# Seven half products: the order of weight sums, sums of h and reads of the products

## The chip, the cores and the metric

The kernel runs on one core of one Trainium2 chip. The metric is the device time of one execution in microseconds (us), taken as the median of the runs. TensorE (PE) does the matrix products and transposes, VectorE (DVE) and ScalarE (ACT) the elementwise work, GpSimd (POOL) and SyncE (SP) mostly issue DMAs. Each engine works through its own queue in order.

## What is computed

```python
def _attn_ref(q, k, v):                       # 4 batches, 12 heads, 448 rows, width 64
    scores = scale * np.matmul(q, k.transpose(0, 1, 3, 2)) - np.log(S)
    attn = 1.0 / (1.0 + np.exp(-scores))
    return np.matmul(attn, v)

def _moe_ref(x, w1, w2, w3, w_out):           # 1792 tokens, 768 -> 768
    h = np.maximum(np.maximum(x @ w1, x @ w2), x @ w3)
    return h @ w_out

def _moe2_ref(x, modality_id, w_gate, modality_bias, w1, w2):
    logits = x @ w_gate + modality_bias[modality_id]
    e_idx = np.argmax(logits, axis=1)         # one of 8 experts for each token
    ...
    h = np.maximum(x[mask] @ w1[e], 0.0)      # 768 -> 1024
    out[mask] = gate_w[mask, None] * (h @ w2[e])   # 1024 -> 768
```

The three stages follow each other. The change lies in the last one, the experts.

## The kernel before

**Tiles and steps.** The last stage sorts the tokens by expert into four token tiles of 512, 512, 448 and 384 rows (the loop over `todo`, tile `i` = 0 to 3). Each tile uses one expert. In tiles 0 to 2 a tile is 26 steps `n`. Steps 0 to 11 are the first layer (`mm1`): four groups `q` of three steps, each group one quarter of h in a PSUM accumulator `hacc`. Steps 12 to 25 are the second layer, `h @ w2`, done as seven products of half size (a Strassen-like scheme) instead of eight: product `j` takes steps 12 + 2j and 13 + 2j (`mm2_prod`, tile `oacc`), 12 matmuls a step. The last tile has a plain second layer and isn't touched. All operands are split into a high and a low part (`split`: the high part by ACT in line 188, the low part by DVE in line 189), and each product is high*high + high*low + low*high.

**Operands of the seven products.** `PRODS` names the left factor (a quarter of h or a sum of quarters), the weight factor (a quarter of w2 or a sum of quarters), the PSUM accumulator group, and whether the product starts the group:

```python
SUMS = {"T1": ("B12", "B11"), "T2": ("B22", "T1"), "T3": ("B22", "B12"), "T4": ("B21", "T2")}
PRODS = (("A11", "B11", 0, True), ("S2", "T2", 1, True), ("A12", "B21", 0, False), ("S3", "T3", 1, False),
         ("S1", "T1", 2, True), ("A22", "T4", 3, True), ("S4", "B22", 2, False))
```

The quarters of w2 lie in `raw` and `rawb`; T1, T3 and T4 are written over B11, B12 and B21, T2 into `tw`. Each sum is two DVE subtractions of 128x768 (`make_sum`, line 823). The sums of h come from `half_sums`, called when a group `q` ends: groups 0 and 1 give A11 (high and low) and the start of the sums; groups 2 and 3 give A12, A22, S2 (high and low) and S1, S4 for later. S1, S3, S4 are split later by `split_sum` into the places of S2, A11 and A12.

**Reads.** Groups 0, 1 and 2 of `oacc` take two products each, and the sum is read out after the first (`read_prod(0)`, `(1)`, `(4)`) and again after the second. The second product of a group adds onto the first, so it can't start before the read of the first is done. Reads 0 and 2 are ACT's (lines 936 to 939), reads 1, 3, 4, 5, 6 DVE's (line 943).

**What sets the order.** The order on PE, ACT and DVE is the order of the code. At the end of step `n` the loop does: transposes of the next tile's tokens, if `n` is in `steps` (`gather_T`, lines 788, 796, 797); `split_sum`, if `n - 12` is in `parts`; `read_prod` at even steps from 14 on; the weight split for the step four ahead (`ahead`, `ck_split`); and the weight sums of `make[n]`. Six buffers `wo_ck` hold split weights.

```python
steps = {N1 + 4: 0, N1 + 7: 1, N1 + 10: 2}          # N1 = 12
make = {8: (("T1", 0),), 9: (("T2", 0), ("T1", 1)), 10: (("T2", 1), ("T3", 0)), 11: (("T3", 1),),
        N1 + 1: (("T4", 0),), N1 + 4: (("T4", 1),)}
parts = {2: ("S3", 0), 3: ("S3", 1), 5: ("S1", 0), 6: ("S1", 1), 8: ("S4", 0), 9: ("S4", 1)}
```

The loads of w2 for tiles 1 and 2 are issued on SP in the second layer of the tile before, those for tile 0 at fixed steps of tile 0's first layer (`wl`).

## Time and profile before

| | |
|---|---|
| median of 3 runs | 756.77 us (756.66 to 757.22) |
| profiled execution, its own time | 760.69 us |
| its span, first to last instruction | 758.9 us |
| busy, share of the span | PE 97%, DVE 64%, ACT 35%, POOL 9% |
| second layer of tile 0 | 520.88 to 560.37 us, 39.49 us |
| second layer of tile 1 | 593.05 to 632.64 us, 39.59 us |
| second layer of tile 2 | 662.39 to 702.28 us, 39.89 us |

The page's busy shares are averages over the whole span. The stretches of the table are read from PE's instructions in order of time: each ends where the next tile's first layer begins. A wait in brackets stands at the instruction that ended it, with the instruction that released it; where several were waited for, the name is that of the last by the profile.

### The profile page before, as it was taken

The numbers are of one execution on the slowest core, as the hardware profiler recorded it, in microseconds if no ns is written. First come the engines' busy times: TensorE is split into PE (matmuls) and PEld (weight loads), VectorE is DVE, ScalarE is ACT, GpSimd is POOL, SyncE is SP. The second block draws the span as 40 slices with busy tenths as digits, with TensorE's granted clock in tenths as the row PEclk, the third lists the DMA queues.
The fourth block names the chain that finished last, engine by engine and source line by source line (L and its number), as shares of the span: only waits on it lengthen the run. The fifth ranks groups of instructions, "written<-read, shape, count | busy, mean of one in ns | idle before, by whom it ended". The sixth has DMA issues, their size and how long they took to land.

```text
span 758.9 us, 10678 instructions
## 1 busy us (share of the span) xinstructions
PE 733.0 (97%) x4164; PEld 619.8 (82%) x4164; DVE 486.9 (64%) x845; ACT 262.9 (35%) x410; POOL 71.5 (9%) x96
## 2 busy tenths in 40 slices
PE   9999999999999999999999999998999799979996
PEld 6455544898998989898899888887988798979996
DVE  4777774757968878744156571338953985588463
ACT  5666555001000100100046242434623553365252
POOL 2000000000000000000010034440140013000101
PEclk9999999999999999999999999999999999989999
DMA  8866680132621312200001145483360044405101
GB/s 208 205 170 161 162 226 1 44 124 84 205 85 44 103 64 84 84 2 0 1 15 58 56 127 170 119 281 148 112 223 0 1 144 170 167 1 179 56 1 60
DMA packets 42330, 78.58 MB, mean 104 GB/s; under 512 B 6201, under 2 KB 28794, under 8 KB 42276
## 3 DMA queue, kind: packets, MB, share of 16 engines
q1 hardware_dynamic: 38420, 66.10, 28.3%
q0 software_dynamic: 3776, 11.63, 4.7%
q8 instruction: 35, 0.57, 0.3%
q14 instruction: 19, 0.16, 0.1%
q10 hardware_dynamic: 80, 0.11, 0.0%
HBM read 69.79 MB, written 11.58 MB: 107 GB/s over the span
## 4 chain that ended last, share of the span: by engine, by line
PE 87%; DVE 5%; ACT 3%; issue 2%; DMA 2%; POOL 0%; POOLq 0%; ACTq 0%; SPq 0%; DVEq 0%
PE acc L499 34%; PE hacc L898 13%; PE oacc L924 8%; PE X L344 7%; PE s L318 7%; PE acc_b L563 5%; PE acc_a L563 4%; PE oacc L912 3%; ACT wo_ck L188 2%; PE X L352 1%; PE s L334 1%; PE acc_c L563 1%; DVE wo_ck L189 1%; PE xT L788 1%; DVE hx L863 1%
## 5 line engine op out<-in xcount | busy, mean ns | idle before, releaser
L499 PE MATMUL acc<-xR,w_ring 128*128 128x512 f32 (+1 forms) x864 | 208.2, 362 | 0.0
L499 PEld LDWEIGHTS acc<-xR,w_ring 128*128 128x128 f32 x864 | 157.6, 188 | 17.7 <-issue 0.7
L898 PE MATMUL hacc<-xh,wo_ck 128*128 128x512 f32 (+3 forms) x600 | 121.9, 363 | 0.0
L898 PEld LDWEIGHTS hacc<-xh,wo_ck 128*128 128x128 f32 x600 | 107.2, 188 | 13.3 <-issue 0.3
L924 PE MATMUL oacc<-wo_ck,hx 128*128 128x384 f32 x504 | 99.1, 353 | 15.4 <-ACT wo_ck L188 8.7
L924 PEld LDWEIGHTS oacc<-wo_ck,hx 128*128 128x128 f32 x504 | 92.4, 199 | 19.2 <-ACT wo_ck L188 11.2
L499 PE MATMUL acc<-xLa,w_ring 128*128 128x512 f32 (+1 forms) x360 | 101.3, 362 | 0.0
L301 ACT ACTIVATE at<-s,nlns 128x896 f32<-128x896 f32 x84 | 78.0, 1008 | 44.9 <-PE s L318 43.6
L189 DVE TENSOR_TENSOR wo_ck<-raw,wo_ck 128x512 fp32r<-128x512 f32 (+1 forms) x87 | 67.8, 805 | 25.1 <-ACT wo_ck L188 22.4
L499 PEld LDWEIGHTS acc<-xLa,w_ring 128*128 128x128 f32 x360 | 66.3, 188 | 7.1
L188 ACT ACTIVATE wo_ck<-raw 128x512 fp32r<-128x512 f32 (+1 forms) x87 | 59.8, 725 | 18.5 <-PE oacc L924 9.0
L318 PEld LDWEIGHTS s<-kq 64*128 64x128 f32 x432 | 38.1, 187 | 21.0 <-issue 15.5
L318 PE MATMUL s<-kq 64*128 64x448 f32 x432 | 51.5, 379 | 0.0
L503 ACT ACTIVATE hA<-acc 128x1024 f32<-128x1024 f32 (+1 forms) x8 | 7.4, 923 | 118.3 <-PE acc L499 118.3
L480 DVE SCALAR_TENSOR_TENSOR gk<-wof,gk 128x768 f32<-128x768 f32 x48 | 45.9, 957 | 1.4
L989 POOL MEMSET xo<- 128x544 f32 x5 | 2.6, 550 | 411.4 <-PE acc_a L563 382.9
L775 POOL DMA_INDIRECT xg<-x2d,idx x30 | 31.6, 1053 | 77.5 <-PE xT L788 38.4
L344 PE MATMUL X<-at,u 128*64 128x448 f32 x192 | 37.8, 543 | 0.0
L370 DVE CAST xR<-X 128x448 fp32r<-128x448 f32 x24 | 14.9, 620 | 32.6 <-PE X L352 32.6
L505 DVE TENSOR_TENSOR hB<-hB,acc 128x1024 f32<-128x1024 f32 (+1 forms) x8 | 8.7, 1087 | 39.5 <-PE acc L499 39.4
L188 ACT ACTIVATE w_ring<-cv 128x768 fp32r<-128x768 f32 x14 | 11.8, 841 | 54.7 <-PE acc L499 54.7
L505 DVE TENSOR_TENSOR hA<-hA,acc 128x1024 f32<-128x1024 f32 (+1 forms) x16 | 17.4, 1086 | 20.3 <-PE acc L499 19.9
(259 smaller groups left out, 885.5 us busy)
## 6 DMA issues: line engine op xcount, KB each, us to landing
stage<-in_moe_w_dram SPq DMA_DIRECT2D x18, 768.0 KB
raw<-in_moe_w_dram SPq DMA_DIRECT2D x12, 1024.0 KB
u<-in_qk_dram SPq DMA_DIRECT2D x46, 224.0 KB
raw<-in_moe_w_dram SPq DMA_DIRECT2D x12, 768.0 KB
stage<-in_moe_w_out_dram SPq DMA_DIRECT2D x6, 768.0 KB
x2d<-xo SPq DMA_DIRECT2D x28, 128.0 KB
gk<-wgT SPq DMA_DIRECT2D x8, 384.0 KB
rawb<-in_moe_w_dram SPq DMA_DIRECT2D x4, 768.0 KB
```

What stands on the lines that cost most here:

```text
L188: nc.scalar.activation(out=r(dR), in_=src, func=ACTF.Copy)
L189: nc.vector.tensor_tensor(out=r(dL), in0=src, in1=dR, op=ALU.subtract)
L301: nc.scalar.activation(out=dst, in_=s[:, :, 0:S], func=ACTF.Sigmoid, scale=qscale, bias=nlns)
L318: nc.tensor.matmul(s[g][:, h, 0:S], r(kt[p, a, 0, 128 * g:128 * (g + 1)]), r(kt[p, x, 1]), start=(n == 0), stop=(n == 2))
L344: nc.tensor.matmul(X_t[u][64 * h:64 * h + 64, 0:S], vt[:, 2 * g + h], at[:, 2 * g + h], start=(g == 0), stop=False)
L480: nc.vector.scalar_tensor_tensor(out=junk, in0=wof[kb], scalar=1.0, in1=wgb[e % 2], op0=ALU.mult, op1=ALU.mult, accum_out=gw[:, kb, e:e + 1])
L499: nc.tensor.matmul(acc[:, c, 0:cw], r(m[:, a, kk, :]), r(x[kk][:, c0 + cw * c:c0 + cw * (c + 1)]), start=(kk == 0 and n == 0), stop=(kk == ...
L505: nc.vector.tensor_tensor(out=dst, in0=dst, in1=acc[:, :, 0:cw], op=ALU.max)
L563: nc.tensor.matmul(acc, r(hs[:, a, kk, :]), r(w(kk, b)), start=(kk == 0 and n == 0), stop=(kk == KB - 1 and n == 2))
L775: d = nc.gpsimd.indirect_dma_start(out=xg[s][:, XC[c][0]:XC[c][1]], out_offset=None, in_=x2d[c], in_offset=bass.IndirectOffsetOnAxis(ap=ix ...
L898: st["mm"] = nc.tensor.matmul(acc[:, f, t0:t1], r(w[a][:, k, 128 * f:128 * (f + 1)]), r(x[:, 2 * c + k, t0:t1]), start=(t0 == 0 and c == 0 ...
L924: nc.tensor.matmul(o[:, s, 0:HC], r(hz[k][:, x, 2 * c + f, 128 * s:128 * (s + 1)]), r(w[a][:, f]), start=(first and c == 0 and f == 0 and ...
```

## The change

Four things move; no matmul, split or sum is added or left out.

- `SUMS`: T3 = B22 - B12 comes first, then T2 = T3 + B11, T1 = B22 - T2, T4 = B21 - T2. T3 and T2 no longer need B11's place, so in tiles 1 and 2 they are formed at steps 5 to 7, T1 at steps 9 and 10. In tile 0, T3 and T2 are formed at steps 9 and 10, T1 at 12 and 13. T4 moves from steps 13 and 16 to 17 and 18.
- `half_sums`: for groups 2 and 3 only S2 is formed at once (function `s2`), with ACT's high parts of A12 and A22. The low part of A12, the sums S1 and S4 and the low part of A22 go into the queue `later`: for group 2 it is emptied at once, for group 3 one entry at each of the steps 12 to 15.
- In the second layer's steps the read comes first, then `split_sum`, then one entry of `later`, then the transposes; the transposes move from steps 16, 19, 22 to 19, 21, 23, the split of S4 from 20, 21 to 21, 22.
- Tile 0's loads of w2 are issued one place earlier each.

```diff
-        SUMS = {"T1": ("B12", "B11"), "T2": ("B22", "T1"), "T3": ("B22", "B12"), "T4": ("B21", "T2")}
+        SUMS = {"T3": ("B22", "B12"), "T2": ("T3", "B11"), "T1": ("B22", "T2"), "T4": ("B21", "T2")}
...
-            nc.vector.tensor_tensor(out=d, in0=a, in1=b, op=ALU.subtract)
+            nc.vector.tensor_tensor(out=d, in0=a, in1=b, op=ALU.add if k == "T2" else ALU.subtract)
...
-        hz, hr = {}, {}
+        hz, hr, later = {}, {}, deque()
...
+            def s2():
+                ve_(out=S2[:, :, b_], in0=b, scalar=0.0, in1=S3[:, :, b_], op0=ALU.max, op1=ALU.subtract)
+                if n2 < TH:
+                    nc.vector.tensor_scalar(out=S2[:, :, n2:TH], in0=S3[:, :, n2:TH], scalar1=-1.0, scalar2=None, op0=ALU.mult)
+                act(out=r(z("S2", 0)), in_=S2, func=ACTF.Copy)
+                act(out=r(z("A12", 0)), in_=a, func=ACTF.Relu)
+                act(out=r(z("A22", 0)[:, :, b_]), in_=b, func=ACTF.Relu)
+                nc.vector.tensor_tensor(out=r(z("S2", 1)), in0=S2, in1=z("S2", 0), op=ALU.subtract)
...
-                return
-            act(out=r(z("A12", 0)), in_=a, func=ACTF.Relu)
-            ve_(out=S1[:, :, b_], in0=b, scalar=0.0, in1=S2[:, :, b_], op0=ALU.max, op1=ALU.add)
-            ve_(out=S2[:, :, b_], in0=b, scalar=0.0, in1=S3[:, :, b_], op0=ALU.max, op1=ALU.subtract)
-            if n2 < TH:
-                nc.vector.tensor_scalar(out=S2[:, :, n2:TH], in0=S3[:, :, n2:TH], scalar1=-1.0, scalar2=None, op0=ALU.mult)
-            act(out=r(z("S2", 0)), in_=S2, func=ACTF.Copy)
-            act(out=r(z("A22", 0)[:, :, b_]), in_=b, func=ACTF.Relu)
-            ve_(out=S4, in0=a, scalar=0.0, in1=S2, op0=ALU.max, op1=ALU.subtract)
-            low("A12", a)
-            low("A22", b, n2)
-            nc.vector.tensor_tensor(out=r(z("S2", 1)), in0=S2, in1=z("S2", 0), op=ALU.subtract)
+                return []
+            s2()
+            return [lambda: low("A12", a),
+                    lambda: ve_(out=S1[:, :, b_], in0=b, scalar=0.0, in1=S1[:, :, b_], op0=ALU.max, op1=ALU.add),
+                    lambda: ve_(out=S4, in0=a, scalar=0.0, in1=S2, op0=ALU.max, op1=ALU.subtract),
+                    lambda: low("A22", b, n2)]
...
-                half_sums(q, acc, nt)
+                later.extend(half_sums(q, acc, nt))
+                while q < 3 and later:
+                    later.popleft()()
...
-        steps = {N1 + 4: 0, N1 + 7: 1, N1 + 10: 2}
+        steps = {N1 + 7: 0, N1 + 9: 1, N1 + 11: 2}
...
+        make = [{9: "T3 0 T2 0", 10: "T3 1 T2 1", 12: "T1 0", 13: "T1 1"},
+                {5: "T3 0", 6: "T2 0 T3 1", 7: "T2 1", 9: "T1 0", 10: "T1 1"}]
+        for m in make:
+            m.update({17: "T4 0", 18: "T4 1"})
...
-            if i == 0 and p in (3, 4, 6, 7):
+            if i == 0 and p in (2, 3, 5, 6):
...
+            if not last and n >= N1:
+                if n > N1 and (n - N1) % 2 == 0:
+                    read_prod((n - N1) // 2 - 1, i, ixs[i])
+                if n - N1 in parts:
+                    split_sum(*parts[n - N1])
+                if later:
+                    later.popleft()()
+                if n == NCW - 1:
+                    read_prod(6, i, ixs[i])
             if not last and n in steps:
...
```

The lines below show what stands in DVE's queue. L189 is the low part of a split (`wo_ck` a weight step, `hx` a sum of h), L823 a half of a weight sum, L863 a low part of A11, A12 or A22; `sum` and `sums` are S1 to S4, `raw` and `tw` the weights.

DVE in tile 1, around the end of group 2 of the first layer (the first of L874 to L880), before:

```order
L189 TENSOR_TENSOR wo_ck<-raw,wo_ck 128x512 x3
L874 SCALAR_TENSOR_TENSOR sums<-hacc,sum_3927 128x512
L875 SCALAR_TENSOR_TENSOR sum_3927<-hacc,sums 128x512
L880 SCALAR_TENSOR_TENSOR sum_3926<-hacc,sum_3927 128x512
L863 SCALAR_TENSOR_TENSOR hx_3785<-hacc,hx_3785 128x512
L863 SCALAR_TENSOR_TENSOR hx_3923<-hacc,hx_3923 128x512
L883 TENSOR_TENSOR hx_3784<-sum_3927,hx_3784 128x512
L189 TENSOR_TENSOR wo_ck<-raw,wo_ck 128x768
L823 TENSOR_TENSOR raw<-raw 128x2x384
L189 TENSOR_TENSOR wo_ck<-raw,wo_ck 128x768
L823 TENSOR_TENSOR tw<-raw 128x768
L823 TENSOR_TENSOR raw<-raw 128x2x384
```

The same place now; group 2 ends at L866:

```order
L189 TENSOR_TENSOR wo_ck<-raw,wo_ck 128x512
L823 TENSOR_TENSOR raw<-raw 128x2x384
L189 TENSOR_TENSOR wo_ck<-raw,wo_ck 128x512
L823 TENSOR_TENSOR tw<-raw 128x768
L823 TENSOR_TENSOR raw<-rawb,raw 128x2x384
L189 TENSOR_TENSOR wo_ck<-raw,wo_ck 128x512
L823 TENSOR_TENSOR tw<-raw 128x768
L866 SCALAR_TENSOR_TENSOR sum_3927<-hacc,sums 128x512
L872 TENSOR_TENSOR hx_3784<-sum_3927,hx_3784 128x512
L863 SCALAR_TENSOR_TENSOR hx_3785<-hacc,hx_3785 128x512
L884 SCALAR_TENSOR_TENSOR sums<-hacc,sums 128x512
L885 SCALAR_TENSOR_TENSOR sum_3926<-hacc,sum_3927 128x512
```

The four operations of T3 and T2 have moved ahead of the end of group 2, between the weight splits of the first layer.

DVE in tile 1, around the first DVE read of the second layer (L943, read 1), before:

```order
L823 TENSOR_TENSOR raw<-raw,tw 128x2x384
L189 TENSOR_TENSOR hx_3783<-sums,hx_3783 128x512
L189 TENSOR_TENSOR wo_ck<-raw,wo_ck 128x768
L189 TENSOR_TENSOR hx_3783<-sums,hx_3783 128x512
L189 TENSOR_TENSOR wo_ck<-raw,wo_ck 128x768
L797 TENSOR_TENSOR xh<-xT,xh 128x2x256 x2
L943 SCALAR_TENSOR_TENSOR xo<-oacc,gcol,xo 128x384 x2
L189 TENSOR_TENSOR wo_ck<-raw,wo_ck 128x768
```

The same place now; the read is L948:

```order
L189 TENSOR_TENSOR hx_3783<-sums,hx_3783 128x512
L885 SCALAR_TENSOR_TENSOR sum_3926<-hacc,sum_3927 128x512
L189 TENSOR_TENSOR wo_ck<-raw,wo_ck 128x768
L189 TENSOR_TENSOR hx_3783<-sums,hx_3783 128x512
L863 SCALAR_TENSOR_TENSOR hx_3923<-hacc,hx_3923 128x512
L189 TENSOR_TENSOR wo_ck<-raw,wo_ck 128x768
L948 SCALAR_TENSOR_TENSOR xo<-oacc,gcol,xo 128x384 x2
L189 TENSOR_TENSOR wo_ck<-raw,wo_ck 128x768
```

The transposed tokens (L797) and T4 (the first row before) no longer stand ahead of the read; two of the put-off operations of group 3 (L885, L863) do.

DVE in tile 0, from the weight split of step 15 to the split of S3, before:

```order
L189 TENSOR_TENSOR wo_ck<-tw,wo_ck 128x768
L823 TENSOR_TENSOR raw<-rawb,raw 128x2x384
L189 TENSOR_TENSOR wo_ck<-raw,wo_ck 128x768
L189 TENSOR_TENSOR wo_ck<-rawb,wo_ck 128x768
L823 TENSOR_TENSOR raw<-raw,tw 128x2x384
L189 TENSOR_TENSOR hx_3783<-sums,hx_3783 128x512
```

The same place now:

```order
L189 TENSOR_TENSOR wo_ck<-tw,wo_ck 128x768
L863 SCALAR_TENSOR_TENSOR hx_3785<-hacc,hx_3785 128x512
L189 TENSOR_TENSOR wo_ck<-raw,wo_ck 128x768
L823 TENSOR_TENSOR raw<-raw,tw 128x2x384
L884 SCALAR_TENSOR_TENSOR sums<-hacc,sums 128x512
L189 TENSOR_TENSOR wo_ck<-rawb,wo_ck 128x768
L823 TENSOR_TENSOR raw<-rawb,tw 128x2x384
L189 TENSOR_TENSOR hx_3783<-sums,hx_3783 128x512
```

In tile 0 both halves of T1 stand here, where the second half of T3 and the first of T4 stood; L863 and L884 are put-off operations of group 3.

## Rows read from the trace of the kernel before

**Rows 1.** The page, part 1: busy us, share of the span, instructions.
```profile
PE 733.0 (97%) x4164; PEld 619.8 (82%) x4164; DVE 486.9 (64%) x845; ACT 262.9 (35%) x410; POOL 71.5 (9%) x96
```

**Rows 2.** Waits of PE from 500 us: total us, times, longest.
```profile
PE oacc L924 <- ACT wo_ck L188: 8.7, 8, 2.0
PE oacc L924 <- DVE wo_ck L189: 6.0, 3, 2.0
PE oacc L924 <- DVE xo L943: 0.7, 1, 0.7
```

**Rows 3.** PE in order of time, second layer of tile 1: start us, busy us, instruction.
```profile
593.05 6.43 PE L924 MATMUL oacc<-wo_ck,hx 128*128 128x384 f32 x36
601.34 0.61 PE L924 MATMUL oacc<-wo_ck,hx 128*128 128x384 f32 x2 [1.85 <-ACT wo_ck L188]
603.99 5.63 PE L924 MATMUL oacc<-wo_ck,hx 128*128 128x384 f32 x22 [2.05 <-DVE wo_ck L189]
609.46 1.03 PE L788 MATMUL xT<-ident,xg 128*128 128x128 f32 x8
610.26 2.35 PE L924 MATMUL oacc<-wo_ck,hx 128*128 128x384 f32 x12
613.22 4.40 PE L924 MATMUL oacc<-wo_ck,hx 128*128 128x384 f32 x24 [0.61 <-ACT wo_ck L188]
...
628.40 4.40 PE L924 MATMUL oacc<-wo_ck,hx 128*128 128x384 f32 x24 [0.68 <-ACT wo_ck L188]
632.64 29.91 PE L898 MATMUL hacc<-xh,wo_ck 128*128 128x448 f32 x144
```

**Rows 4.** PE in order of time, ends of the second layers of tiles 0 and 2.
```profile
520.88 6.43 PE L924 MATMUL oacc<-wo_ck,hx 128*128 128x384 f32 x36
...
560.37 32.84 PE L898 MATMUL hacc<-xh,wo_ck 128*128 128x512 f32 x144
...
662.39 6.41 PE L924 MATMUL oacc<-wo_ck,hx 128*128 128x384 f32 x36
...
702.28 25.12 PE L898 MATMUL hacc<-xh,wo_ck 128*128 128x384 f32 x144
```

**Rows 5.** Stretches: length, busy of PE, PEld, DVE, ACT, POOL, PEclk, DMA share, GB/s.
```profile
604.00:606.00 2.00, 2.00 (x6) 2.00 (x7) 2.00 (x3) 2.00 (x5) 0.00 (x0) 0.50 0.00 0
482.00:484.20 2.20, 0.46 (x5) 0.22 (x3) 0.63 (x2) 0.00 (x0) 1.40 (x1) 1.00 0.87 258
```

**Rows 6.** DVE in order of time, tile 1.
```profile
588.33 0.69 DVE L880 SCALAR_TENSOR_TENSOR sum<-hacc,sum 128x512 f32<-128x512 f32 x1 [1.19 <-ACT hx L879]
588.93 1.28 DVE L863 SCALAR_TENSOR_TENSOR hx<-hacc,hx 128x512 fp32r<-128x512 f32 x2
...
592.59 0.95 DVE L189 TENSOR_TENSOR wo_ck<-raw,wo_ck 128x768 fp32r<-128x768 f32 x1
593.46 0.95 DVE L823 TENSOR_TENSOR tw<-raw 128x768 f32<-128x768 f32 x1
...
602.99 0.95 DVE L189 TENSOR_TENSOR wo_ck<-tw,wo_ck 128x768 fp32r<-128x768 f32 x1
...
611.94 1.13 DVE L943 SCALAR_TENSOR_TENSOR xo<-oacc,gcol,xo 128x384 f32<-128x384 f32 x2
```

**Rows 7.** ACT in order of time, tile 1.
```profile
585.09 0.60 ACT L873 ACTIVATE hx<-hacc 128x512 fp32r<-128x512 f32 x1 [5.51 <-PE hacc L898]
...
599.44 0.63 ACT L878 ACTIVATE hx<-sum 128x512 fp32r<-128x512 f32 x1 [3.60 <-DVE sum L875]
...
600.45 0.83 ACT L188 ACTIVATE wo_ck<-tw 128x768 fp32r<-128x768 f32 x1
```

**Rows 8.** The same places in tile 0 (ACT) and tile 2 (DVE).
```profile
512.76 0.60 ACT L873 ACTIVATE hx<-hacc 128x512 fp32r<-128x512 f32 x1 [1.12 <-PE hacc L898]
...
650.74 1.90 DVE L189 TENSOR_TENSOR wo_ck<-raw,wo_ck 128x512 fp32r<-128x512 f32 x3 [0.86 <-ACT wo_ck L188]
```

**Rows 9.** A stretch of tile 1's first layer, columns as in Rows 5.
```profile
570.00:575.00 5.00, 5.00 (x24) 4.14 (x23) 2.98 (x5) 1.42 (x3) 0.00 (x0) 1.00 0.00 0
```

More of the change, by code (lines that the diff above doesn't have):

```diff
@@ L863, in low @@
                 ve_(out=r(z(k, 1)[:, :, 0:n]), in0=src, scalar=0.0, in1=z(k, 0)[:, :, 0:n], op0=ALU.max, op1=ALU.subtract)
+            def s2():
[6 more added lines that the diff above has]
+                nc.vector.tensor_tensor(out=r(z("S2", 1)), in0=S2, in1=z("S2", 0), op=ALU.subtract)
             if q < 2:
-                act(out=S2[:, :, b_], in_=b, func=ACTF.Relu)
+                act(out=S1[:, :, b_], in_=b, func=ACTF.Relu)
                 act(out=r(z("A11", 0)), in_=a, func=ACTF.Relu)
-                ve_(out=S3[:, :, b_], in0=acc[:, :, b_], scalar=0.0, in1=S2[:, :, b_], op0=ALU.max, op1=ALU.subtract)
+                ve_(out=S3[:, :, b_], in0=acc[:, :, b_], scalar=0.0, in1=S1[:, :, b_], op0=ALU.max, op1=ALU.subtract)
                 low("A11", a)
@@ L1106, in attn_moe_kernel @@
         early = []
-        steps = {N1 + 4: 0, N1 + 7: 1, N1 + 10: 2}
-        make = {8: (("T1", 0),), 9: (("T2", 0), ("T1", 1)), 10: (("T2", 1), ("T3", 0)), 11: (("T3", 1),),
-                N1 + 1: (("T4", 0),), N1 + 4: (("T4", 1),)}
-        parts = {2: ("S3", 0), 3: ("S3", 1), 5: ("S1", 0), 6: ("S1", 1), 8: ("S4", 0), 9: ("S4", 1)}
+        steps = {N1 + 7: 0, N1 + 9: 1, N1 + 11: 2}
[3 more added lines that the diff above has]
+            m.update({17: "T4 0", 18: "T4 1"})
+        parts = {2: ("S3", 0), 3: ("S3", 1), 5: ("S1", 0), 6: ("S1", 1), 9: ("S4", 0), 10: ("S4", 1)}
         for p, (i, n) in enumerate(todo):
@@ L1160, in attn_moe_kernel @@
                     keep_gate(i + 1, SH // 128 if i + 1 == NF else NB)
-            if not last and n >= N1:
-                if n - N1 in parts:
-                    split_sum(*parts[n - N1])
-                if n > N1 and (n - N1) % 2 == 0:
-                    read_prod((n - N1) // 2 - 1, i, ixs[i])
-                if n == NCW - 1:
-                    read_prod(6, i, ixs[i])
             ahead(p + 1 + LA)
-            for k in () if last else make.get(n, ()):
-                make_sum(*k)
+            m = [] if last else make[min(i, 1)].get(n, "").split()
+            for k, c in zip(m[::2], m[1::2]):
+                make_sum(k, int(c))
             if i == NF - 2 and n == NCW - 1:
```

## The prediction

> **What bounds the kernel now.** I read the page's busy shares first, then PE's waits, then PE, DVE and ACT in order of time through one second layer, then the clock. PE is busy 97% of the span [rows 1], so only its waits, and matmuls at a low clock, can be won back. From 500 us on PE waits 15.4 us in all, every time at the second layer's matmuls (L924) [rows 2]. Each of the three changed tiles has the same four waits; tile 1 shows them [rows 3]. After 36 matmuls it waits 1.85 us and, two matmuls later, 2.05 us: step 15 needs the high and then the low part of its weights, T2, which ACT and DVE deliver at 601.28 and 603.94 [rows 6, 7]. Then 0.61 us at step 18 and 0.68 us at step 24. The profile names ACT there, but the work that fits is a read: step 18 adds onto the accumulator that read 1 empties, that read ends at 611.94 + 1.13 = 613.07 [rows 6], and PE starts 0.15 us later; the read stands behind the transposed tokens in DVE's queue.
>
> A fifth loss is no wait. The 22 matmuls after the second wait take 609.46 - 603.99 = 5.47 us; the last 24 of the stage take 632.64 - 628.40 = 4.24, or 0.1767 each, by which 22 take 3.89. [...] That costs 1.6 us.
>
> **What there is to win.** A second layer is 168 matmuls, 29.7 us at 0.1767, and three transposes of 0.80 (609.46 to 610.26), 32.1 in all. Tile 1 takes 632.64 - 593.05 = 39.6, tile 0 39.5, and tile 2, whose transposes are three quarters as large (an estimate, 1.8 for the three, 31.5 in all), 39.9 [rows 3, 4]. So 7.5, 7.4 and 8.4 us are lost, **23.3 us** together. This is more than the 15.4 of waits because of the clock and because each restart costs some 0.2 us beyond the wait shown.
>
> **The change, part by part.** Instruction counts stay, so the question is when DVE, now the last to deliver, gets to the things that PE needs. I follow its queue by hand, with the times from one start to the next: 0.60 us for an operation of 512 columns (588.33 to 588.93), 0.87 for one of 768 (592.59 to 593.46) [rows 6], and two ACT operations in 1.01 (599.44 to 600.45) [rows 7].
>
> *Sums of weights early, tile 1.* T3 and T2 are four operations of 0.87, 3.5 us, put among the first layer's splits. Group 2 ends at 585.09 [rows 7], and DVE has room before it (in the stretch of [rows 9] it is busy 2.98 of 5 us), so the first layer's matmuls hide them. What they need is loaded: no DMA moves from 570 to 575, and the first sum comes at about 580. If that cover were gone, each us of a late load would be a us for the splits queued behind it, and PE waits for those.
>
> *Only S2 at once.* From 585.09: L866 0.69, ACT's copy 0.63, L872 at 586.46. The low part of A12 must then wait for both of ACT's reads of the accumulator (1.01 for the copy and the first, 0.6 for the second), to 587.43. L880 shows that: it uses nothing that ACT's L879 writes, yet is released by it [rows 6]. [...]
>
> On from 587.43: four operations of 0.60, then two splits and two halves of T1 with step 14's split between them, 5 x 0.87: group 3's L866 starts at 594.18. S2 is ready for ACT at 594.90; three ACT operations (1.51) and step 15's high part (0.83) end at 597.24; its low part runs 597.26 to 598.2. PE wants step 15 at 593.05 + 36 x 0.1767 = 599.4. **The two large waits go**, with 1.2 us to spare, and with them the low clock.
>
> *Late next: read 1.* From 597.26 DVE has the splits of steps 15 to 19 (5 x 0.87) and six operations of 0.60 (put-off parts of group 3 and the two halves of S3), some 0.05 of waits between: read 1 starts at 605.26, ends 1.13 later at 606.39, and step 18 starts at 606.53. PE is ready at 593.05 + 72 x 0.1767 = 605.77, so it waits **0.8 us**. Step 24's wait goes: its read comes before the transposes and 1 us before PE. The stage loses 0.8 instead of 7.5.
>
> *Tile 2.* DVE is later here. Step 9's low part starts at 650.74 [rows 8]; three splits of 0.60 and the four new sums of 0.87 end at 656.02, about 1 us after group 2 does (three steps of 29.91 / 12 before 662.39 [rows 3, 4]). Walked on in the same way (some operations of this shorter tile take 0.47), step 15's weights come at 668.7, as PE wants them (662.39 + 6.36), and read 1 lets PE on at 676.83. PE is ready at 662.39 + 12.72 = 675.11: it waits **1.7 us** instead of losing 8.4.
>
> *Tile 0.* Here T3 and T2 stay between groups 2 and 3 and T1 falls between step 15 and read 1. From 512.76 [rows 8] the same walk gives step 15's low part at 527.87 (T2 waits for T3, the split of T2 for ACT), then 5 x 0.87 + 6 x 0.60 + 2 x 0.87 for T1: read 1 from 537.56, step 18 at 538.83. PE is ready at 520.88 + 12.72 = 533.60: it still loses **5.2 us** of its 7.4. Part falls at step 15, the last stretch is some 3 us without a break. Does the clock fall? It fell after 1.85 and 2.05 us of waiting with two matmuls between [rows 3]; it stayed at full after a single wait of 1.75 us at 482 [rows 5] and after all of the short ones. Three us is nearer to the first, so I take a fall and its 1.6 us; from the other row it is nothing.
>
> *At nothing.* Transposes, put-off parts, T4 and the split of S4 have 2 us or more before the step that needs them. POOL has to issue four scatters of tile 0 ahead of the last gather for tile 2, which PE uses some 50 us later. Tile 0's loads start a step earlier (32.84 / 12 = 2.7 us [rows 4]) and share the DMA queues with the gathers there: between nothing and those 2.7 us, taken at nothing, since PE waits for no gather in that tile now [rows 2].
>
> **The sum.** Lost after: 5.2 + 1.6 + 0.8 + 1.7 = 9.3 of 23.3, so **14.0 us** gained. The profiled execution took 760.69 us (758.9 of span), which gives 746.7; the median of the runs is 756.77, which gives **742.8 us**.
>
> **The rivals.**
> - *Every wait closes.* DVE reaches read 1 before PE in all three tiles: 23.3 us, 733.5. For it: in tile 1 only 0.8 us is missing. Against: in tile 0 5 us are, and nothing in the queue gets shorter.
> - *DVE falls further behind.* Tiles 1 and 2 leave no slack in DVE from the end of group 2 to read 1. If each restart there costs 1 us more and the clock falls in both (2 x 1.6), 5.2 us of the gain go: 748.0. For it: tile 2's step 15 has nothing to spare. Against: single waits under 2 us left the clock alone [rows 5].
> - *Slower: the early sums wait for loads.* T3 in tiles 1 and 2 needs the last of w2 at 580, some 13 us before the first T2 did (593.46 [rows 6]). If a load landed later than the sum's turn at 580, the splits of steps 10 to 12 would stand behind it and the first layer would stop. The kernel gets slower when loads land more than 7 us after that in tile 1 and alike in tile 2, which eats the 14.0 us; at 10 us each, it would be 756.77 - 14.0 + 20 = 762.8. Against: DMA is still at 570 [rows 9].
> - *It changes nothing that counts:* the waits return whole behind other operations, 756.8. Against: the queue has 3.5 us less before read 1, and the transposes are out of its way.
>
> **How the numbers follow.** Forecast 742.8 (740 to 746, the clock in tile 0 and 1 us of read 1 either way): 0.62. Every wait closes: 0.11. Further behind (746 to 750): 0.20. Slower: 0.03. No change: 0.04. The range 737 to 749 holds the forecast, nearly all of the second rival and the gap towards the first; outside lie the first, the slower one and no change, 0.18. Faster by over 0.2%, which is about what a measurement of this kernel can tell from none (below 755.3): 0.93; within 0.2%: 0.04; slower: 0.03.
>
> **What would show it.** Right: in tiles 1 and 2 no wait at step 15, granted clock 1.00 throughout, one wait of 0.5 to 2 us at step 18, released soon after DVE's first read; the read at about 606 (tile 1); none at step 24; second layers of 33 to 34 us in tiles 1 and 2 and 37 to 39 in tile 0, with one wait of some 3 us at step 18 there, and a clock of 0.50 behind it. Wrong: waits in the first layer (late loads), a wait at step 15 in tile 1 (ACT's queue was misread), or a read 1 that PE doesn't wait for.

## The result

The changed kernel takes **743.74 us** (median of 4 runs, 743.2 to 744.5), the kernel before beside it 756.71 (756.35 to 757.22): a ratio of 0.9829, 95% interval 0.9812 to 0.9846, 13.0 us faster. The forecast was 742.8 in a range of 737 to 749. The profiled execution took 743.39 us, its span 741.6.

The page's first part of the kernel after, as [rows 1]. PE's busy time fell by 6.5 us, although it runs the same 4164 matmuls:

```profile
PE 726.5 (98%) x4164; PEld 615.7 (83%) x4164; DVE 486.7 (66%) x845; ACT 262.9 (35%) x410; POOL 70.4 (9%) x96
```

What PE waits for from 470 us on, as [rows 2] (total us, times, longest). 15.4 us have become 7.3, and most of it is what the prediction named as next: read 1, now line L948, three times.

```profile
PE oacc L929 <- DVE xo L948: 5.4, 3, 3.1
PE oacc L929 <- ACT wo_ck L188: 0.9, 1, 0.9
PE oacc L929 <- ACT xo L942: 0.6, 2, 0.3
PE oacc L929 <- DVE wo_ck L189: 0.4, 1, 0.4
```

PE in order of time through the three second layers (tiles 0, 1, 2), as [rows 3, 4] (start us, busy us, instruction, idle time before it and its releaser; L929 was L924, L901 was L898):

```profile
517.18 6.43 PE L929 MATMUL oacc<-wo_ck,hx 128*128 128x384 f32 x36
524.51 0.62 PE L929 MATMUL oacc<-wo_ck,hx 128*128 128x384 f32 x2 [0.90 <-ACT wo_ck L188]
525.50 2.01 PE L929 MATMUL oacc<-wo_ck,hx 128*128 128x384 f32 x10 [0.37 <-DVE wo_ck L189]
527.86 4.46 PE L929 MATMUL oacc<-wo_ck,hx 128*128 128x384 f32 x24 [0.34 <-ACT xo L942]
535.45 5.96 PE L929 MATMUL oacc<-wo_ck,hx 128*128 128x384 f32 x24 [3.14 <-DVE xo L948]
...
556.40 32.84 PE L901 MATMUL hacc<-xh,wo_ck 128*128 128x512 f32 x144
589.08 12.67 PE L929 MATMUL oacc<-wo_ck,hx 128*128 128x384 f32 x72
602.61 4.40 PE L929 MATMUL oacc<-wo_ck,hx 128*128 128x384 f32 x24 [0.86 <-DVE xo L948]
...
622.02 29.91 PE L901 MATMUL hacc<-xh,wo_ck 128*128 128x448 f32 x144
651.77 8.49 PE L929 MATMUL oacc<-wo_ck,hx 128*128 128x384 f32 x48
660.49 4.43 PE L929 MATMUL oacc<-wo_ck,hx 128*128 128x384 f32 x24 [0.22 <-ACT xo L942]
666.28 4.40 PE L929 MATMUL oacc<-wo_ck,hx 128*128 128x384 f32 x24 [1.36 <-DVE xo L948]
...
684.99 25.12 PE L901 MATMUL hacc<-xh,wo_ck 128*128 128x384 f32 x144
```

In tile 1 the stage starts with 72 matmuls without a break, steps 12 to 17; then comes one wait of 0.86. In tile 0 the broken start and the long wait at step 18 remain, and the 24 matmuls behind that wait take 5.96 us instead of 4.40. The lengths of the stages (from one L929 start to the next L901 start):

| second layer, us | before | after | gained | predicted gain |
|---|---|---|---|---|
| tile 0 | 39.49 | 39.22 | 0.27 | 7.4 - 6.8 = 0.6 |
| tile 1 | 39.59 | 32.94 | 6.65 | 6.7 |
| tile 2 | 39.89 | 33.22 | 6.67 | 6.7 |
| sum | 118.97 | 105.38 | **13.59** | **14.0** |

The profiled executions differ by 760.69 - 743.39 = 17.30, the medians by 12.97. The other 3.70 us lie ahead of tile 0's second layer (520.88 before, 517.18 after): the profile of before has a wait of 1.75 us for a gather at 484 and three stalls at 466 to 468 that the profile of after lacks. An experiment below shows that these are not the change's. So the stages are what is compared here.

The groups of these matmuls by line, before and after, say how the gain divides (busy us, mean ns | idle time before them and its releasers): 15.4 - 7.2 = 8.2 us of waits and 99.1 - 93.7 = 5.4 us of busy time, together the 13.6. Of the 5.4, 4.2 us are the lower clock: before, the 22 matmuls behind the second wait took 5.65, 5.63 and 6.71 us in the three tiles, at a granted clock of 0.70 in tile 0 (531.6 to 537.2 us), 0.50 in tile 1 (604 to 606 us [rows 5]) and 0.50 in tile 2 (673.3 to 677 us), against 4.08 at a granted clock of 1.00 (601 to 605 us in the first experiment below), and after, 1.56 are lost in tile 0. The other 1.2 would be the restarts, 12 before and 7 after; that is not shown.

```profile
L924 PE MATMUL oacc<-wo_ck,hx 128*128 128x384 f32 x504 | 99.1, 353 | 15.4 <-ACT wo_ck L188 8.7 <-DVE wo_ck L189 6.0 <-DVE xo L943 0.7
```

```profile
L929 PE MATMUL oacc<-wo_ck,hx 128*128 128x384 f32 x504 | 93.7, 341 | 7.2 <-DVE xo L948 5.4 <-ACT wo_ck L188 0.9 <-ACT xo L942 0.6
```

Stretches of the kernel after, columns as in [rows 5]: in tile 1, around its wait, the clock stays at 1.00; in tile 0, behind the 3.14 us, it is 0.57 in the mean (0.50 from 536 to 538 us). DVE works without a pause in both (4.00 of 4.00).

```profile
602.00:606.00 4.00, 3.39 (x20) 3.42 (x21) 4.00 (x6) 1.59 (x4) 0.00 (x0) 1.00 0.37 98
535.00:539.00 4.00, 3.55 (x12) 3.58 (x13) 4.00 (x6) 0.40 (x1) 0.00 (x0) 0.57 0.42 117
```

DVE of the kernel after in tile 1, as [rows 6]: the last halves of T3 and T2 among the weight splits; then the end of group 2, a put-off part of group 3, and read 1.

```profile
578.22 0.95 DVE L823 TENSOR_TENSOR raw<-rawb,raw 128x768 f32<-128x768 f32 x1
579.09 0.68 DVE L189 TENSOR_TENSOR wo_ck<-raw,wo_ck 128x512 fp32r<-128x512 f32 x1
579.69 0.95 DVE L823 TENSOR_TENSOR tw<-raw 128x768 f32<-128x768 f32 x1
581.12 0.69 DVE L866 SCALAR_TENSOR_TENSOR sum<-hacc,sums 128x512 f32<-128x512 f32 x1 [0.48 <-PE hacc L901]
...
583.48 0.69 DVE L863 SCALAR_TENSOR_TENSOR hx<-hacc,hx 128x512 fp32r<-128x512 f32 x1 [0.28 <-ACT hx L871]
...
593.31 0.96 DVE L189 TENSOR_TENSOR wo_ck<-tw,wo_ck 128x768 fp32r<-128x768 f32 x1 [1.01 <-ACT wo_ck L188]
...
599.86 0.68 DVE L863 SCALAR_TENSOR_TENSOR hx<-hacc,hx 128x512 fp32r<-128x512 f32 x1
600.46 0.95 DVE L189 TENSOR_TENSOR wo_ck<-raw,wo_ck 128x768 fp32r<-128x768 f32 x1
601.33 1.14 DVE L948 SCALAR_TENSOR_TENSOR xo<-oacc,gcol,xo 128x384 f32<-128x384 f32 x2
```

DVE has 0.48 us of room before group 2 ends, so the early sums cost nothing in this tile; no sum waits for a load. Tile 2 has no such room: there the sums end about 1 us behind group 2, and L866 follows them at 645.41 without a pause. Read 1 ends at 602.47 and PE starts at 602.61, 0.14 later (0.15 in the profile of before).

### The profile page after: what moved, and what is told of

The parts are those of the page before. It is cut to its first block, busy times and chain, and to the rows that moved or that the text cites. A ratio compares the mean times of both kernels' runs of the same rounds, so it can differ in the third digit from the quotient of the medians.

```text
span 741.6 us, 10670 instructions
## 1 busy us (share of the span) xinstructions
PE 726.5 (98%) x4164; PEld 615.7 (83%) x4164; DVE 486.7 (66%) x845; ACT 262.9 (35%) x410; POOL 70.4 (9%) x96
## 4 chain that ended last, share of the span: by engine, by line
PE 88%; DVE 7%; ACT 2%; issue 1%; POOL 0%; POOLq 0%; ACTq 0%; DVEq 0%
PE acc L499 35%; PE hacc L901 12%; PE X L344 8%; PE oacc L929 7%; PE s L318 7%; PE acc_b L563 5%; PE acc_a L563 4%; PE oacc L917 3%; PE acc_c L563 3%; DVE wo_ck L189 2%; PE X L352 1%; PE xT L788 1%; PE s L334 1%; DVE raw L823 1%; DVE hx L863 1%
## 5 line engine op out<-in xcount | busy, mean ns | idle before, releaser
L901 PE MATMUL hacc<-xh,wo_ck 128*128 128x512 f32 (+3 forms) x600 | 121.9, 363 | 0.0
L901 PEld LDWEIGHTS hacc<-xh,wo_ck 128*128 128x128 f32 x600 | 107.2, 188 | 13.3 <-issue 0.3
L929 PE MATMUL oacc<-wo_ck,hx 128*128 128x384 f32 x504 | 93.7, 341 | 7.2 <-DVE xo L948 5.4
L929 PEld LDWEIGHTS oacc<-wo_ck,hx 128*128 128x128 f32 x504 | 88.5, 191 | 9.5 <-issue 4.6
L189 DVE TENSOR_TENSOR wo_ck<-raw,wo_ck 128x512 fp32r<-128x512 f32 (+1 forms) x87 | 68.1, 805 | 24.2 <-ACT wo_ck L188 24.2
L370 DVE CAST xR<-X 128x448 fp32r<-128x448 f32 x24 | 14.8, 619 | 32.1 <-PE X L352 32.1
```

The source lines that it names most:

```text
L189: nc.vector.tensor_tensor(out=r(dL), in0=src, in1=dR, op=ALU.subtract)
L901: st["mm"] = nc.tensor.matmul(acc[:, f, t0:t1], r(w[a][:, k, 128 * f:128 * (f + 1)]), r(x[:, 2 * c + k, t0:t1]), start=(t0 == 0 and c == 0 ...
L929: nc.tensor.matmul(o[:, s, 0:HC], r(hz[k][:, x, 2 * c + f, 128 * s:128 * (s + 1)]), r(w[a][:, f]), start=(first and c == 0 and f == 0 and ...
```

## The experiments

The theory: DVE is the last to deliver, and each tile's loss is the time by which its queue reaches step 15's weights, and then read 1, later than PE. The rivals: the transposes and the order of the reads bring the gain; the putting off does; the clock does it all and the waits matter little. Each kernel is compared with the kernel before run beside it on the same occasion, or by the lengths of its stages. There were four occasions: 760.21 us for the kernel before on the first (each part alone, and one more operation), 757.69 on the second (the changed kernel again, and the first three versions that take work from in front of read 1), 757.83 on the third (the change without the putting off, the old loads, and the last version), 760.77 on the fourth (the kernel before, profiled again).

### One part of the change alone

Only the sums early (`SUMS`, `make` and the loads as after, the rest as before):

```diff
-        SUMS = {"T1": ("B12", "B11"), "T2": ("B22", "T1"), "T3": ("B22", "B12"), "T4": ("B21", "T2")}
+        SUMS = {"T3": ("B22", "B12"), "T2": ("T3", "B11"), "T1": ("B22", "T2"), "T4": ("B21", "T2")}
...
+                {5: "T3 0", 6: "T2 0 T3 1", 7: "T2 1", 9: "T1 0", 10: "T1 1"}]
```

> The kernel before with only the new weight sums (order of T3, T2, T1, T4, their steps, and tile 0's loads one place earlier); sums of h, reads and transposes as before. Theory (DVE's queue decides): in tiles 1 and 2 the queue has 3.5 us less between group 2 and step 15, so the two waits at step 15 shrink from 3.9 us to one of about 1.4 and the low clock behind them goes; the waits of about 0.6 at steps 18 and 24 stay, since the reads still stand behind the transposed tokens. Gain about 4 us in each of tiles 1 and 2, 0 to 1 in tile 0: 748 us. Rival (ACT's high parts decide step 15, as the profile names ACT): ACT still gets its two reads of group 3 late, so the waits stay and the time is 755 or more. Second rival (the sums are all that counts): 743.7, as after.

Measured: 750.57 us, ratio 0.9868 (0.9852 to 0.9884), 9.6 us faster. Its stages take 39.62, 35.12 and 34.59. PE in tile 1:

```profile
593.14 6.78 PE L924 MATMUL oacc<-wo_ck,hx 128*128 128x384 f32 x38
601.17 4.08 PE L924 MATMUL oacc<-wo_ck,hx 128*128 128x384 f32 x22 [1.24 <-DVE wo_ck L189]
...
608.84 4.40 PE L924 MATMUL oacc<-wo_ck,hx 128*128 128x384 f32 x24 [0.60 <-ACT wo_ck L188]
```

Of the two waits of 1.85 and 2.05 [rows 3] one of 1.24 is left, the 22 matmuls behind it run at a granted clock of 1.00 (4.08 us instead of 5.63; 601 to 605 us), and the wait of 0.60 at step 18 stays as it was. The wait that bore ACT's name is gone though ACT's work is the same. Nothing changed in tile 0, where T2 is formed no earlier than before. So the sums carry some 10 of the 13 us, waits and clock together.

Only the reads first and the transposes later (`steps`, `parts` and the order within a step as after, the rest as before):

```diff
-        steps = {N1 + 4: 0, N1 + 7: 1, N1 + 10: 2}
+        steps = {N1 + 7: 0, N1 + 9: 1, N1 + 11: 2}
...
+                if n > N1 and (n - N1) % 2 == 0:
+                    read_prod((n - N1) // 2 - 1, i, ixs[i])
                 if n - N1 in parts:
                     split_sum(*parts[n - N1])
-                if n > N1 and (n - N1) % 2 == 0:
-                    read_prod((n - N1) // 2 - 1, i, ixs[i])
```

> The kernel before with only the order of the second layer's steps changed: read first, transposes at steps 19, 21, 23, split of S4 one step later; weight sums and sums of h as before. Theory (a DVE read, not ACT's weights, is what steps 18 and 24 wait for): both short waits go, step 15's two waits and the low clock stay: about 1.7 us for each tile, 751.5 us. Rival (ACT's weight splits, as the profile names them): the waits at 18 and 24 stay, within 1 us of 756.7.

Measured: 755.92 us, ratio 0.9940 (0.9924 to 0.9957), 4.3 us faster. Its stages take 37.74, 38.76 and 37.96. The waits of 0.6 at steps 18 and 24 are gone in all three tiles, the pair at step 15 is as before. PE in tiles 0 and 1:

```profile
531.51 11.97 PE L924 MATMUL oacc<-wo_ck,hx 128*128 128x384 f32 x58 [2.04 <-DVE wo_ck L189]
...
602.09 12.82 PE L924 MATMUL oacc<-wo_ck,hx 128*128 128x384 f32 x58 [2.04 <-DVE wo_ck L189]
```

58 matmuls behind a single wait take 10.35 us (a row of the change without the putting off, below): those behind the pair of waits lose 1.6 here and 2.5 there. The clock was not read in these stretches; over the whole execution its mean is 0.986, against 0.993 in the variant of that row. That the clock costs those 1.6 and 2.5 is an estimate from these figures. That the profile named ACT as the releaser of the waits at steps 18 and 24 was wrong. Step 18's own weights were split long before; DVE in tile 1 of the kernel before:

```profile
607.93 0.95 DVE L189 TENSOR_TENSOR wo_ck<-raw,wo_ck 128x768 fp32r<-128x768 f32 x1
```

This low part, the second of the two, is done at 608.88, over 4 us before PE starts at 613.22; the split of ACT that ends just ahead of that (613.17) is one for a later step. What was not run apart is the read first and the transposes later: both take the transposed tokens out of the read's way.

Only the putting off (`s2` and `later`, the rest as before):

```diff
-                half_sums(q, acc, nt)
+                later.extend(half_sums(q, acc, nt))
+                while q < 3 and later:
+                    later.popleft()()
```

> The kernel before with only the sums of h changed: S2 at once, the rest of group 3 put off over steps 12 to 15; weight sums, reads and transposes as before. Theory (DVE's queue): step 15's low part comes about 2.9 us earlier in each tile, but what was put off and all six sums still stand ahead of read 1, behind the transposed tokens, so most of the gain is given back at step 18: about 1 us for each tile, 753 to 754 us. Rival (what PE waits for at step 15 is all there is to win): 3.9 us of wait and 1.6 of clock in each tile, 743 us or less.

Measured: 759.27 us (757.02 to 763.22 in 10 runs), ratio 0.9987 (0.9970 to 1.0004): no difference that can be told; the gain of 1 us for each tile did not come. PE in tile 1, from step 15 on, in the profiled execution, the slowest of the ten:

```profile
601.03 0.62 PE L929 MATMUL oacc<-wo_ck,hx 128*128 128x384 f32 x2 [0.74 <-ACT wo_ck L188]
602.02 2.01 PE L929 MATMUL oacc<-wo_ck,hx 128*128 128x384 f32 x10 [0.38 <-DVE wo_ck L189]
...
613.17 7.11 PE L929 MATMUL oacc<-wo_ck,hx 128*128 128x384 f32 x24 [2.94 <-DVE xo L948]
```

Step 15 waits 0.74 and 0.38 instead of 1.85 and 2.05, but the parts that were put off now stand before read 1, which step 18 awaits for 2.94 us, and the 24 matmuls behind this one wait take 7.11 us instead of 4.40. The mean granted clock of this execution is 0.990, that of the fastest of the ten (757.02 us) 0.999. The wait was moved, not removed: PE's waits in tile 1 are 5.6 us in all, 5.2 before. To see whether this holds with the other parts in place, the change without its putting off (`half_sums` as before, `later` taken out, all else as after):

> The changed kernel with one part undone: all sums of h of group 3 at once, as before the change (no S2 first, nothing put off); new weight sums, reads first. Theory (DVE's queue): putting off only moves the wait between step 15 and step 18. Tiles 1 and 2 lose 1.3 to 1.5 us at step 15 again (as the run with the new weight sums alone showed), but read 1 then comes before PE wants it: second layers of about 33.5 us instead of 32.9 and 33.2. Tile 0 waits at step 15 with the low clock and not at step 18: about 37.8 instead of 39.2. In all within 1 us of the changed kernel. Rival (S2 at once is what removes the large waits): 4 to 5 us slower in each tile, 755 or so.

Measured: 742.88 us, ratio 0.9800 (0.9784 to 0.9817), 14.95 us below its before. The changed kernel was 13.0 below, and 13.7 when it was run a second time (744.04, ratio 0.9820, 0.9804 to 0.9836), with this expected of that run:

> The changed kernel itself, run beside the next three for a comparison on one chip. Both theories: 13 us faster than the kernel before of this chip, whatever that takes; second layers of 39.2, 32.9 and 33.2 us in tiles 0, 1 and 2.

The intervals overlap, and the stages sum to 104.94 us against 105.38: the putting off brings nothing that can be measured. PE in tiles 0 and 1:

```profile
528.00 12.76 PE L924 MATMUL oacc<-wo_ck,hx 128*128 128x384 f32 x58 [2.04 <-DVE wo_ck L189]
...
596.45 10.35 PE L924 MATMUL oacc<-wo_ck,hx 128*128 128x384 f32 x58 [1.25 <-DVE wo_ck L189]
```

Tile 1 waits 1.25 once at step 15 and not at step 18, instead of 0.86 at step 18. DVE does the same work before read 1 either way.

The earlier loads of tile 0, undone:

```diff
-            if i == 0 and p in (2, 3, 5, 6):
+            if i == 0 and p in (3, 4, 6, 7):
```

> The changed kernel with tile 0's loads of w2 at their old places. Theory (loads have room): T3 and T2 are formed at the same time, 743.7 us, tile 0's second layer 39.2. Rival (the sums at steps 9 and 10 need the earlier loads): DVE waits for a DMA before the second half of T3, and tile 0 loses up to 2.7 us more.

Measured: 743.07 us (741.4 to 744.77), ratio 0.9813 (0.9791 to 0.9835): as after. No sum waits for a load. In its profiled execution tile 0's wait is the same 3.13 us as in the kernel after, but the 24 matmuls behind it take 4.40 us instead of 5.96, and the mean granted clock of the execution is 0.999 (0.997 in the kernel after):

```profile
535.08 4.40 PE L929 MATMUL oacc<-wo_ck,hx 128*128 128x384 f32 x24 [3.13 <-DVE xo L948]
```

### One more operation in DVE's queue

If DVE's queue sets the time of read 1, one operation of 768 columns more in front of it (the first half of T1 formed a second time, with the same values, at step 13) must cost its 0.87 us in each tile and nothing else:

```diff
-        make = [{9: "T3 0 T2 0", 10: "T3 1 T2 1", 12: "T1 0", 13: "T1 1"},
-                {5: "T3 0", 6: "T2 0 T3 1", 7: "T2 1", 9: "T1 0", 10: "T1 1"}]
+        make = [{9: "T3 0 T2 0", 10: "T3 1 T2 1", 12: "T1 0", 13: "T1 1 T1 0"},
+                {5: "T3 0", 6: "T2 0 T3 1", 7: "T2 1", 9: "T1 0", 10: "T1 1", 13: "T1 0"}]
```

> The changed kernel with one DVE operation of 0.87 us more in each of tiles 0 to 2, between step 15's split and read 1 (the first half of T1 is formed a second time at step 13, the same values). Theory (DVE's queue sets step 18): step 18 starts 0.87 us later in each tile, 2.6 us in all: 746.3 us, and the waits at step 18 read 4.0, 1.7 and 2.2 us. Rival (another engine or a wait sets step 18 and DVE has slack): 743.7, waits as they were.

Measured: 750.73 us, ratio 0.9871 (0.9854 to 0.9887): 9.5 us below its before instead of 13.0 to 13.7, so 3.5 to 4.2 us slower than the changed kernel. Its step 18 in the three tiles:

```profile
540.24 5.88 PE L929 MATMUL oacc<-wo_ck,hx 128*128 128x384 f32 x24 [4.03 <-DVE xo L948]
...
608.12 4.40 PE L929 MATMUL oacc<-wo_ck,hx 128*128 128x384 f32 x24 [1.66 <-ACT hx L188]
...
672.45 5.99 PE L929 MATMUL oacc<-wo_ck,hx 128*128 128x384 f32 x24 [2.00 <-DVE xo L948]
```

The waits grew by 0.89, 0.80 and 0.64, the stages by 0.80, 0.79 and 2.26. What tile 2 lost beyond the theory is the clock, which in tile 2 fell behind the longer wait: 5.99 us for 24 matmuls at a granted clock of 0.64 (672 to 676 us); in tile 0 it is 5.88 at 0.57 (540 to 544 us). This is the clearest reading of the study: what stands in front of read 1 on DVE is paid for nearly one to one, and now and then some 1.6 us more. The rival that puts all on the clock falls here: tile 1 lost its 0.79 at a granted clock of 1.00 (608 to 612 us).

### Taking work from in front of read 1

Read 1 issued at the start of step 15 instead of 16, one weight split, one split of S3 and one put-off part earlier in DVE's queue:

```diff
-                if n > N1 and (n - N1) % 2 == 0:
+                if n == N1 + 3:
+                    read_prod(1, i, ixs[i])
+                elif n > N1 and n != N1 + 4 and (n - N1) % 2 == 0:
```

> The changed kernel with read 1 issued at step 15 instead of 16, ahead of the second half of S3's split, of one put-off operation and of step 19's weight split in DVE's queue (0.60 + 0.60 + 0.87 = 2.07 us). Theory (DVE's queue sets step 18): the waits at step 18 of 0.9 and 1.4 us in tiles 1 and 2 go, that of 3.1 us in tile 0 shrinks to 1.1; second layers of 32.1, 31.8 and, in tile 0, 37.1 or 35.6 if the low clock there goes with the wait. 4.3 to 5.9 us faster than the changed kernel. Rival (step 18 waits for the split of S3 or for its weights, and the read only comes at the same time): the order then puts the split of step 19 later, and nothing is gained: within 1 us of the changed kernel.

Measured: 738.11 us, ratio 0.9742 (0.9726 to 0.9758), 5.9 us below the changed kernel run beside it; stages 36.22, 31.83 and 32.06. PE at tile 0's step 18, and at the start of tile 1's second layer:

```profile
534.01 4.42 PE L929 MATMUL oacc<-wo_ck,hx 128*128 128x384 f32 x24 [1.09 <-ACT xo L944]
...
586.67 16.83 PE L929 MATMUL oacc<-wo_ck,hx 128*128 128x384 f32 x96
```

Tile 1 now runs 96 matmuls without a wait: the rival "every wait closes" has come true there, by a further step. In tile 0 the wait falls from 3.16 in the run beside it to 1.09, by the three operations that the read was moved past (0.60 + 0.60 + 0.87 = 2.07), and the 24 matmuls behind it take 4.42 us instead of 5.98 (the mean granted clock of the execution is 0.999, of the one beside it 0.995). The named releaser is ACT's read 2 (L944), of another accumulator group than step 18's, but DVE's read 1, of step 18's own, ends at 532.73 + 1.14 = 533.87, again 0.14 before PE:

```profile
532.73 1.14 DVE L948 SCALAR_TENSOR_TENSOR xo<-oacc,gcol,xo 128x384 f32<-128x384 f32 x2
```

Can the rest of tile 0 be won by moving T1 behind read 1 as well (`15: "T1 0", 16: "T1 1"` in the place of 12 and 13)?

> As the run before, and in tile 0 T1 is formed at steps 15 and 16 instead of 12 and 13, so behind read 1. Theory: tile 0 has another 1.74 us less ahead of read 1; its wait at step 18 goes, and with it the low clock; second layer of tile 0 34.0 us, the others as in the run before. 7 to 7.5 us faster than the changed kernel. Rival (the clock falls in tile 0 for the short waits at steps 15 and 16 alone): 35.6 us in tile 0.

It can't: 739.64 us, ratio 0.9762 (0.9746 to 0.9779), 1.5 us slower than with read 1 alone. The wait at step 18 is gone and comes back behind it:

```profile
537.30 5.38 PE L929 MATMUL oacc<-wo_ck,hx 128*128 128x384 f32 x24
543.82 1.25 PE L788 MATMUL xT<-ident,xg 128*128 128x128 f32 x8 [1.14 <-DVE xh L797]
...
551.01 4.42 PE L929 MATMUL oacc<-wo_ck,hx 128*128 128x384 f32 x24 [0.90 <-DVE xo L948]
```

T1 now stands with T4 ahead of the transposed tokens and a later read, and steps 20 and 21 (the 24 matmuls from 537.30) take 5.38 us instead of 4.42; what slows them is not shown (the mean granted clock of the execution is 0.997, that with read 1 alone 0.999). In tile 0 DVE has no pauses between steps 14 and 24 but its waits for ACT (here 1.00, 0.39 and 0.37 us from 534 to 552 us); work moved within this stretch was paid for at its end. The kernel after shows the first of these waits, DVE in tile 0: the low part of T2 stands right behind T2, and waits for ACT to split it.

```profile
516.74 0.96 DVE L823 TENSOR_TENSOR tw<-raw 128x768 f32<-128x768 f32 x1
518.66 0.96 DVE L189 TENSOR_TENSOR wo_ck<-tw,wo_ck 128x768 fp32r<-128x768 f32 x1 [0.97 <-ACT wo_ck L188]
```

So T3 and T2 one step earlier (`8: "T3 0 T2 0", 9: "T3 1 T2 1"`), beside the late T1:

> As the run before, and in tile 0 T3 and T2 are formed at steps 8 and 9 instead of 9 and 10, so that step 14's split no longer waits for its sum in DVE's queue (1 us of idle DVE there). Theory: step 15's waits of 0.9 and 0.4 us in tile 0 shrink to 0.2 or less and read 0 no longer holds step 16; second layer of tile 0 32.6 us: 8.5 to 9 us faster than the changed kernel, a little over 21 us faster than the kernel before. Rival (tile 0's loads of w2 land too late for sums a step earlier): step 15 as in the run before, or worse, and a wait of DVE for DMA before the sums.

738.67 us, ratio 0.9758 (0.9738 to 0.9777): tile 0 takes 36.79 instead of 37.89. DVE's wait for ACT is gone, its low part of T2 comes without a pause:

```profile
518.88 0.96 DVE L823 TENSOR_TENSOR tw<-raw 128x768 f32<-128x768 f32 x1
519.76 0.95 DVE L189 TENSOR_TENSOR wo_ck<-tw,wo_ck 128x768 fp32r<-128x768 f32 x1
```

PE's 0.92 at step 15 went with it. The 0.37 behind it and the late waits stayed, and the 32.6 us expected of the stage were missed by far. So the last version takes the two edits that helped, read 1 at step 15 and T3 and T2 at steps 8 and 9, and leaves T1 at 12 and 13:

> The changed kernel with read 1 at step 15 and, in tile 0, T3 and T2 at steps 8 and 9 (T1 stays at 12 and 13). Theory: the run with T1 late showed that it only moves the wait behind step 18, and the earlier T3 and T2 were worth 1.1 us; so this should be that much faster than read 1 at step 15 alone: second layer of tile 0 35.2 us, tiles 1 and 2 31.8 and 32.1; 7 us faster than the changed kernel, 20 faster than the kernel before. Rival (step 18's other operands hold tile 0): 36.2 us, as with read 1 at step 15 alone.

737.45 us (737.19 to 737.61), ratio 0.9730 (0.9714 to 0.9746): 20.4 us faster than before, stages 35.18, 31.83 and 32.07, the expected ones to 0.1. It is the lowest median of all; its interval overlaps that of read 1 at step 15 alone, but its tile 0 is 1.04 shorter. What is left is 3.3 us in tile 0 (35.18 - 31.83, what tile 1 takes without a wait) and two waits of 0.2 in tile 2.

### The 3.7 us ahead of the stages

The kernel before, profiled again:

> The kernel before, unchanged, profiled once more. In its first profile (760.69 us, 3.9 above its median) PE reached the second layer of tile 0 at 520.88, through a wait of 1.75 for a gather and three short stalls; the changed kernel's profile shows neither and reaches it at 517.18. Theory: those 3.7 us belong to the chip or the execution. Then this profile either has them again and an execution of about 760, or lacks them, reaches tile 0's second layer at about 517 and takes 756 to 758; in both cases the three second layers last 39.5, 39.6 and 39.9, within 0.5. Rival: the change itself removes the gather wait and the stalls. Then they are here whatever the time, and an execution of 757 us has its second layers at 520.9 and is shorter somewhere behind.

Measured: 760.66 us in the profiled execution, a median of 760.04 (ratio 0.9996, 0.9979 to 1.0013), and PE's waits ahead of tile 0's second layer are there once more:

```profile
PE acc_c L563 <- issue: 1.7, 2, 0.8
PE xT L788 <- DMA xg<-x2d,idx: 1.4, 1, 1.4
```

The same waits in the variant with one more DVE operation, which has all of the change, on the occasion on which the kernel before took 760.21:

```profile
PE xT L788 <- DMA xg<-x2d,idx: 1.2, 1, 1.2
PE acc_c L563 <- issue: 1.2, 3, 0.6
```

It reached tile 0's second layer at 521.09; the kernel after reached it at 517.18, and at 517.74 in its second run. The other profiles divide in the same way: the three others of the first occasion reach it at 520.73 to 520.85, the six others of the second and third at 516.80 to 517.85. And the first instruction that the change moves, a load for tile 0, is issued at 489.09 in the kernel after, behind the place of these waits. So the change does not take them away; they go with the occasion. Where they come from stays open, and no execution of the kernel before at 757 us was profiled, so that it lacks them is argued, not shown. The stages of this profile take 40.74, 39.65 and 38.72: in tile 1 as in the first profile, but 1.25 longer in tile 0 and 1.17 shorter in tile 2, more than the 0.5 expected, with a sum of 119.11 against 118.97.

## Why the prediction was right

*Tile 1.* The walk through DVE's queue gave step 18 at 606.53, 13.48 us after the stage's start, with a wait of 0.8; measured 602.61 - 589.08 = 13.53 and 0.86. No wait at step 15, none at step 24, a granted clock of 1.00 from 589.08 to 622.02 us. The step that a look at the data alone would have got wrong is the low part of A12, which waits for both of ACT's reads of the accumulator: it does (0.28 us released by L871, whose result it does not use; 0.17 in tile 2). The base of 32.1 us was 0.3 too long, for tile 1 takes 31.83 without a wait (read 1 at step 15), and the loss was 32.94 - 31.83 = 1.1 and not 0.8, the wait and its restart; the two cancel.

*Tile 2.* Step 18 at 14.44 after the start, with 1.7 us lost; measured 666.28 - 651.77 = 14.51, and 0.22 + 1.36 in two waits. The walk put the 0.22 at read 1 too; it is ACT's read 0 at step 16. The lengths agree to 0.1. That the gain does too, 6.67 against 6.7, is in part luck: the 8.4 lost before held 2.6 us of low clock (22 matmuls in 6.71 us instead of 4.08, 0.50 granted from 673.3 to 677 us), which the second profile of the kernel before has at 1.5 (5.54). By the second profiles of both kernels the gains are 1.48, 6.71 and 5.47, 13.66 in all.

*Tile 0.* Step 18 at 17.95; measured 535.45 - 517.18 = 18.27, for DVE's queue ran 0.3 later from step 15's low part on. Lost there 39.22 - 32.1 = 7.1 instead of 6.8, which puts the stage just outside the 37 to 39 given as a sign, as 32.94 is just outside the 33 to 34 of tile 1. The wait of "some 3 us without a break" was 3.14, and the clock fell as chosen (0.57 from 535 to 539 us). But this choice was between 0 and 1.6 us, and both ends occur: the second run of the kernel after shows a stage of 39.26 (24 matmuls in 5.98 us), the variant with the old loads 37.68 (4.40 us) after the same wait. The term should have stood in the sum as an open one; that it was there in the kernel after's profile is luck.

*The sum.* 13.59 in the stages against 14.0, 12.97 between the medians. The prediction took the gain from the median of the runs and not from the profiled execution (746.7), which turned out right: the 3.9 us by which the profiled execution stands above that median are about the 3.70 that the two profiles differ by ahead of the changed stages.

*At nothing.* The early loads, the early sums in tile 1 and POOL's order cost nothing, as shown by the variant with the old loads, by the 0.48 us of room before group 2 ends, and by the list of PE's waits, in which no load and no gather stands. In tile 2 the early sums make DVE late, as the walk had it. The rival "slower" had no ground. What the prediction did not say is how the gain divides: it costed "only S2 at once" as a step on the way to step 15, and without it the change gains as much.

## What to carry to other kernels

When one engine's queue is the last to deliver to several points in a row, walk the queue to each of them: an operation put off past the first point stands before the second, and the time is the same (743.74 us with the putting off, 742.88 without). Only work moved into a stretch where that engine has room (here the sums of tile 1 and most of those of tile 2, ahead of the end of group 2), or idle time taken from it (its waits for ACT), is won. Look then for the one operation that the next wait needs and put it as early as its data allow: read 1 a step earlier gave 5.9 us, almost half as much as the whole change, some 1.6 of it in tile 0 by the matmuls behind the wait (4.42 us instead of 5.98).
